# A long convolution beside attention on one core: two channels by 64 time shifts on the 128 rows of a filter tile, in place of one channel by 128

## The chip, the core and the metric

The kernel runs on one core of a Trainium2 chip. The metric is the device time of one execution in microseconds (us). In a profile, PE is the matrix engine, PEld its weight loads, DVE the vector engine, ACT the scalar engine, POOL the third compute engine and SP the engine that issues most DMAs. The profile counts 16 DMA engines for the core. "Granted clock" is the share of full clock that PE was allowed. SBUF is the core's working memory, whose tiles here have up to 128 partitions, PSUM the one that PE writes its results to. Repeated runs of one kernel lie up to some 1.5% apart (the fast runs of the kernel before, on the chip of runs 1 to 8, from 859.12 to 871.35 us), so effects of 1% rest on several runs of both kernels on the same chip, with a 95% interval; runs that were marked slow (over 1.5% above the fastest of the same kernel) are left out of the ratios.

## The reference, cut to what matters

Two independent halves, written side by side into one output:

```python
# A: attention, S = 2048, D = 512, 32 heads of 16
qkv = (x @ wqkv) ...
p = softmax(einsum("bhqd,bhkd->bhqk", q, k) * 16 ** -0.5)
a = einsum("bhqk,bhkd->bhqd", p, v) ... @ wo
# B: gated long convolution, 512 channels, filter as long as the sequence
k_shift = ...                     # k filtered in time with 4 taps per channel
kv = k_shift * v
y  = irfft(rfft(kv, 2 * S) * rfft(ssm_k, 2 * S))[:S]     # causal convolution along time
y  = y + kv * ssm_D
b  = q * y
return concatenate([a, b], axis=-1)
```

The kernel does the convolution without an FFT, as matrix products with Toeplitz matrices of the filter. The inputs are small random numbers, and the comparison with the reference is tolerant, so it cannot vouch for the values of the convolution. Where a variant is called correct below, that is by its construction.

## The kernel before

The kernel gives every engine a fixed stream of instructions, and a small model in the kernel's own Python decides the order. A score block is 128 keys by 512 queries. Of 2048 blocks ACT exponentiates 1835 and DVE 213 with a polynomial. Convolution matmuls are slipped between the score matmuls. The model books each DMA at 400 KB per us, plus 3.6 us:

```python
def dma(eng, dsem, outp, inp, deps=(), transpose=False, kb=512):
    h = dsem.add()
    start = max(eng.t, at(*deps))
    dma_t[0] = max(dma_t[0] + kb / DMA_KB, start + 3.6 + kb / DMA_KB)   # DMA_KB = 400
    done[(id(h[0]), h[1])] = dma_t[0]
    ...
```

The filters, reversed and padded with 128 zeros, lie in a DRAM scratch `kz` with one row of LKZ = 2176 elements per channel. A load gives partition p the row shifted by p elements, which makes the Toeplitz tile of a channel. One load serves a quad of four channels:

```python
WR = sb("WR", [128, 12, S])                  # 12 filter rows of 4 KB per partition: 3 slots of 4
KV = sb("KV", [128, C // 4, NB, 4])          # k*v by 128-blocks of time, NB = 16
...
src = bass.AP(tensor=kz_ap.tensor, offset=kz_ap[4 * qd, 0].offset,
              ap=[[1, 128], [LKZ, 4], [1, S]])            # [step, count], outermost first
h_wr[qd] = dma(sp, d_wr[i], WR[:, 4 * i:4 * i + 4, :], src, [h_kzw[0], dep], kb=2048)
...
def conv_lags(qd, n0, n1):                   # 16 lags of 128 times
    for n in range(n0, n1):
        for c in range(4):
            e.matmul(PS[32 * c:32 * c + NB - n, ...], lhsT=KV[:, qd, n:NB, c],
                     rhs=WR[:, r + c, 128 * (NB - 1 - n):128 * (NB - n)],
                     start=(n == 0), stop=(n == NB - 1), tile_position=(0, 32 * c))
    ...
    if n1 == NB:                             # the quad is done: its slot is free, load the next one
        wr_free.append((wr_slot[qd], h))
        load_wr()
```

An access pattern here is a list of [step, count] pairs, the outermost first.

The softmax here doesn't subtract the row's maximum and nothing guards it: scores larger than these inputs give would overflow.

## Time and profile before

| | before |
|---|---|
| time, three runs | 865.52 us (863.67 to 869.0) |
| span of the profiled run | 863.0 us |
| ACT busy | 837.7 us, 97% |
| DMA, MB moved by SP's queue | 279.33 |

ACT fills the span, and the DMA engines are nearly as full once the convolution runs (a share of 0.99 from 200 to 850 us, below). The prediction shows the lines for that. Two more views are used later. The first is from the page: the queue that carries the filter rows (packets, MB, share of the 16 engines' time), and the chain of work that ended last, by engine.

```profile
q1 hardware_dynamic: 93280, 279.33, 84.9%
...
ACT 56%; DMA 21%; PE 12%; DVE 8%; issue 1%; SPq 1%; ACTq 0%
```

The second is ACT's exponentials by stage: the stretch in us, its length, ACT's busy time in exponentials with their count, granted clock, DMA share of 16 engines, GB/s. Before 44 us the filter is prepared, up to 200 us the projections and k*v products are slipped in, and after that convolution and attention run side by side.

```profile
0.00:44.00 44.00, 33.59 (x30) 1.00 1.07 271
44.00:200.00 156.00, 155.30 (x151) 0.99 0.49 172
200.00:850.00 650.00, 639.57 (x557) 0.98 0.99 385
```

Since ACT is the bound, a change is judged by what ACT gets done in each stage. Ten us are lost in the first, only 0.7 in the second, and 10.4 in the third.

### The profile page before, as it was taken

What the parts mean: (1) busy time and instruction counts of PE and PEld (TensorE: products, weight loads), DVE (VectorE), ACT (ScalarE), POOL (GpSimd) and SP (SyncE); (2) the same over time, 40 slices, a digit from 0 to 9 for tenths busy, and PEclk for the clock granted to TensorE, in tenths of its full rate; (3) what the DMA queues carried; (4) which work ended last, traced back from release to release, by engine and by line L of the source; (5) the groups of instructions that cost most, each with busy time, mean ns of one, the idle gap of its engine ahead of it and who ended that gap; (6) DMA issues with size and microseconds to landing.
All of it is one profiled execution on the core that took longest, in us unless ns stands there. A gap on an engine that the chain in (4) does not pass through costs nothing.

```text
span 863.0 us, 29010 instructions
## 1 busy us (share of the span) xinstructions
PE 742.5 (86%) x13170; PEld 301.2 (35%) x13170; DVE 782.5 (91%) x1330; ACT 837.7 (97%) x746; POOL 17.3 (2%) x33
## 2 busy tenths in 40 slices
PE   8988999998888888888888888888888888788876
PEld 2223343443333333333333333333333333333332
DVE  3228999999999999999999999999999989999992
ACT  6999999999999999999999999999999999999997
POOL 2000000000000000000000001000000000000000
PEclk9999999999999999999999999999999999999999
DMA  9960067779999999999999999999999999999972
GB/s 272 269 221 1 1 198 246 261 246 355 407 375 369 404 409 407 405 378 408 407 394 378 407 406 388 356 375 362 385 396 408 406 387 373 392 401 373 408 297 74
DMA packets 98666, 289.31 MB, mean 335 GB/s; under 512 B 29040, under 2 KB 31088, under 8 KB 98160
## 3 DMA queue, kind: packets, MB, share of 16 engines
q1 hardware_dynamic: 93280, 279.33, 84.9%
q0 software_dynamic: 1808, 6.29, 2.2%
q8 instruction: 104, 1.70, 0.8%
q10 hardware_dynamic: 3456, 1.84, 0.7%
q14 instruction: 18, 0.15, 0.0%
HBM read 276.83 MB, written 6.42 MB: 328 GB/s over the span
## 4 chain that ended last, share of the span: by engine, by line
ACT 56%; DMA 21%; PE 12%; DVE 8%; issue 1%; SPq 1%; ACTq 0%
ACT PT L545 56%; DMA WR<-kz_scratch 20%; PE PS L534 5%; DVE EH L588 3%; PE PS L798 3%; PE PS L627 2%; DVE FX L581 1%; DVE PTD L593 1%; DMA WR<-in_B_ssm_D_dram 1%; SPq L218 1%; DVE QT L375 1%; PE PS L744 1%; PE PS L330 0%; PE PS L1004 0%; PE PS L358 0%
## 5 line engine op out<-in xcount | busy, mean ns | idle before, releaser
L545 ACT ACTIVATE PT<-PS 128x1536 bf16<-128x1536 f32 (+1 forms) x741 | 834.6, 1334 | 12.7 <-PE PS L534 11.7
L534 PE MATMUL PS<-QT,KTo 32*128 32x512 bf16 x2048 | 304.1, 388 | 86.9 <-ACT PT L545 69.0
L588 DVE SCALAR_TENSOR_TENSOR EH<-EH,FX 128x512 f32<-128x512 f32 x426 | 282.7, 682 | 0.1
L798 PE MATMUL PS<-WR,KV 128*16 128x128 bf16 (+15 forms) x8192 | 220.7, 222 | 18.1 <-DMA WR<-kz_scratch 16.0
L627 PE MATMUL PS<-PT,VAF 128*32 128x512 bf16 x1835 | 203.8, 393 | 3.7 <-DVE DT L691 2.1
L798 PEld LDWEIGHTS PS<-WR,KV 128*13 128x13 bf16 (+15 forms) x8192 | 148.9, 88 | 102.8 <-issue 40.2
L534 PEld LDWEIGHTS PS<-QT,KTo 32*128 32x128 bf16 x2048 | 73.0, 91 | 268.2 <-ACT PT L545 228.9
L581 DVE TENSOR_SCALAR FX<-PS 128x512 f32<-128x512 f32 x213 | 146.0, 685 | 7.5 <-PE PS L534 6.9
L593 DVE SCALAR_TENSOR_TENSOR PTD<-EH,FX 128x512 uint16<-128x512 f32 x213 | 144.1, 679 | 0.0
L588 DVE SCALAR_TENSOR_TENSOR EH<-FX 128x512 f32<-128x512 uint16 x213 | 143.2, 684 | 0.0
L627 PEld LDWEIGHTS PS<-PT,VAF 128*32 128x32 bf16 x1835 | 49.0, 93 | 120.8 <-issue 105.3
L1004 PE MATMUL PS<-IDN,ZW 128*32 128x512 bf16 (+3 forms) x221 | 70.7, 320 | 0.9 <-issue 0.9
L627 PE MATMUL PS<-PTD,VAF 128*32 128x512 bf16 x213 | 62.2, 387 | 0.0
L400 DVE CAST VAF<-PS 128x512 bf16<-128x512 f32 x16 | 11.1, 691 | 27.9 <-PE PS L358 27.9
L691 DVE STREAM_TRANSPOSE DT<-PS 128x512 f32<-128x512 f32 x31 | 22.0, 711 | 14.1 <-PE PS L627 13.8
L1004 PEld LDWEIGHTS PS<-IDN,ZW 128*32 128x32 bf16 x221 | 21.6, 98 | 8.6 <-issue 8.1
L375 DVE TENSOR_SCALAR QT<-PS,MASK 128x512 bf16<-128x512 f32 x30 | 21.1, 746 | 3.5 <-PE PS L330 3.5
L813 DVE CAST YB<-PS 128x512 bf16<-128x512 f32 x32 | 21.9, 684 | 0.9 <-PE PS L798 0.7
L744 PE MATMUL PS<-WKV,OTN 128*128 128x512 bf16 x64 | 20.1, 392 | 1.2 <-DVE OTN L713 1.2
L358 PE MATMUL PS<-WKV,xT 128*128 128x512 bf16 x64 | 18.8, 384 | 2.3 <-DVE VAF L400 1.7
L339 PE MATMUL PS<-xT,WKV 128*128 128x512 bf16 (+1 forms) x64 | 18.2, 377 | 1.1 <-DVE QT L375 0.5
L330 PE MATMUL PS<-xT,WQ 128*128 128x512 bf16 x60 | 18.0, 384 | 0.2
(62 smaller groups left out, 197.0 us busy)
## 6 DMA issues: line engine op xcount, KB each, us to landing
WR<-kz_scratch SPq DMA_DIRECT2D x128, 2048.0 KB, 11.6
kz_scratch<-WR SPq DMA_DIRECT2D x1, 2176.0 KB, 8.5
WR<-in_B_v_dram SPq DMA_DIRECT2D x4, 512.0 KB, 7.5
QN<-in_B_q_dram POOLq DMA_DIRECT2D x2, 1024.0 KB, 10.8
out_dram<-QN POOLq DMA_DIRECT2D x2, 1024.0 KB, 8.7
out_dram<-OUTA POOLq DMA_DIRECT2D x12, 128.0 KB, 5.7
QN<-in_B_ssm_k_dram SPq DMA_DIRECT2D x1, 1024.0 KB, 6.5
QT<-in_B_ssm_k_dram SPq DMA_DIRECT2D x1, 1024.0 KB, 8.5
```

The source lines that it names most:

```text
L375: lambda e, par=par: e.tensor_scalar(QT[:, qb % 2, 2 * o + par, :], PS[:, bank, :], MASK[:, par:par + 1], None, ALU.mult),
L534: ins = e.matmul(PS[:, bank, :], lhsT=KTo[32 * s:32 * s + 32, g // 2, kt * 128:(kt + 1) * 128], rhs=QT[32 * s:32 * s + 32, qb % 2, g, :], ...
L545: h_exp[T] = act.op(lambda e: e.activation(PT[:, T % R_PT, 0:n * QB], PS[:, banks[0]:banks[0] + n, :].rearrange("p b f -> p (b f)"), ACT.E ...
L581: h_f = urgent(lambda e: e.tensor_scalar(fx, PS[:, bank, :], FIX_ADD, FIX_HI, ALU.add, ALU.min), [h, h_last.get(i - R_FX)], slack=0.6)
L588: st["h"] = dve.op(lambda e: e.scalar_tensor_tensor(eh, src, (A3, A2, A1)[j], frac, ALU.add, ALU.mult), [st["h"], h_last.get(i - R_EH), h_ ...
L593: lambda e: e.scalar_tensor_tensor(out16, eh, A4, fx, ALU.mult, ALU.add),
L627: ins = e.matmul(dst, lhsT=w, rhs=rhs, start=(k == 0), stop=(k == KT - 1), tile_position=(0, 32 * s))
L691: h_t = urgent(lambda e: e.transpose(out=dt, in_=PS[:, pvb(n), :]), [h] + before, slack=0.1, us=(0.63, 0.751))
L744: ins = e.matmul(PS[:, bank, :], lhsT=OTN[:, (4 * qb + o) % R_O, t * 128:(t + 1) * 128], rhs=WO[:, o, :], start=(o == 0), stop=(o == 3))
L798: ins = e.matmul(PS[32 * c:32 * c + NB - n, BGB, 128 * (kk % 4):128 * (kk % 4) + 128], lhsT=KV[:, qd, n:NB, c], rhs=WR[:, r + c, 128 * (NB ...
L813: hh = urgent(lambda e: e.tensor_copy(YB[:, half, :].rearrange("p (k i) -> p k i", k=4), src), [h, h_yb[0]], slack=0.3, us=V512)
L1004: pe.op(lambda e: e.matmul(PS[32 * s:32 * s + 32, pvb(n), 0:128 * k], lhsT=ZW[:, :], rhs=rhs, start=False, stop=False, tile_position=(0, 3 ...
```

## The change

The intent is to halve the bytes of the filter. A filter tile of 128 rows holds 128 shifts of one channel before, 64 shifts of two channels (c and c + 128) after. One matmul then serves two channels, there are 32 lags of 64 times in place of 16 of 128, and each row pair is fetched by one DMA. So that the channels do not mix, the stationary side (k*v) has twice as many columns, and each column is zero in the half of the partitions that belongs to the other channel; its elements lie 4 apart, that is 8 bytes, as before.

```diff
-R_W = 12
+R_W = 10
-    KV = sb("KV", [128, C // 4, NB, 4])
+    KVF = sb("KV", [128, NOCT, 2, 2 * NB, 4])            # NOCT = 64 octets of channels
+    h_kv0 = pool.op(lambda e: e.memset(KVF[:, :, :, :, :], 0.0), [h_vaf1], us=(14.0, 14.1))
+    h_kz0 = pool.op(lambda e: e.memset(KZS[:, :, S:S + PAD], 0.0), [h_kv0])
...
-            h_kvc[c] = hh = urgent(lambda e: e.tensor_tensor(dst, src, val, ALU.mult), ...)
+            for p in range(2):                           # two products on 64 partitions each
+                dst = KV[64 * p:64 * p + 64, ...]
+                h_kvc[c] = hh = urgent(lambda e, ...: e.tensor_tensor(dst, src, val, ALU.mult), ...)
...
-            src = bass.AP(..., offset=kz_ap[4 * qd, 0].offset, ap=[[1, 128], [LKZ, 4], [1, S]])
-            h_wr[qd] = dma(sp, d_wr[i], WR[:, 4 * i:4 * i + 4, :], src, [h_kzw[0], dep], kb=2048)
+            row = 256 * (x // (2 * NOCT)) + x % (2 * NOCT)
+            src = bass.AP(..., offset=kz_ap[row, 0].offset, ap=[[128 * LKZ, 2], [1, 64], [1, S]])
+            h_wr[x] = dma(sp, d_wr[i], WR[:, i, :], src, [h_kzw[0], dep])
...
-                               lhsT=KV[:, qd, n:NB, c],
-                               rhs=WR[:, r + c, 128 * (NB - 1 - n):128 * (NB - n)],
+                               lhsT=KVF[:, od, lag % 2, 2 * q:32, c],
+                               rhs=WR[:, rows[c], w0:w0 + w],
```

Cut are the layout of v and of the copies of y, their smaller transposes, the order of the early units, and the ring of output tiles (4 to 3).

More of the change, by code (lines that the diff above doesn't have):

```diff
@@ L24 @@
 C = 512
+NOCT = C // 8
+NLAG = 32
+LAG_ORDER = [0, -1] + list(range(1, NLAG - 1))
 NB = S // 128
@@ L29 @@
 LKR = LEFT + S
-R_W = 12
+R_W = 10
 R_PT = 5
 R_O = 8
-R_A = 4
+R_A = 3
 CHB = 32
@@ L168, in bass_concat_heads__mha_block__ssm_conv_h3__prompt_kernel @@
     WRF = WR[:, :, :].rearrange("p r w -> p (r w)")
-    KV = sb("KV", [128, C // 4, NB, 4])
+    KVF = sb("KV", [128, NOCT, 2, 2 * NB, 4])
+    KV = KVF[:, :, :, :, :].rearrange("p k r (e h) c -> p r e h k c", h=2)
     QNF = sb("QN", [128, NB * 256 + 2 * LEFT])
@@ L180, in bass_concat_heads__mha_block__ssm_conv_h3__prompt_kernel @@
     OUTA = sb("OUTA", [128, R_A, D])
-    YB = sb("YB", [128, 2, 512])
+    YB = sb("YB", [128, 512])
     IDN = sb("IDN", [128, 128])
@@ L191, in bass_concat_heads__mha_block__ssm_conv_h3__prompt_kernel @@
     WO = WV
-    VST = WR[:, 8:12, :].rearrange("p c (t d) -> p c t d", t=NB)
+    VST = WR[:, 6:10, :].rearrange("p c (r e d) -> p c r e d", r=1, e=NB).rearrange("p (c r) o e d -> p c (r o) e d", r=2)
     KZS = WRF[:, 0:4 * LKZ].rearrange("p (c m) -> p c m", c=4)
@@ L259, in bass_concat_heads__mha_block__ssm_conv_h3__prompt_kernel @@
     d_outA = [DmaSem(sem(f"d_outA{i}")) for i in range(R_A)]
-    d_wr = [DmaSem(sem(f"d_wr{i}")) for i in range(R_W // 4)]
+    d_wr = [DmaSem(sem(f"d_wr{i}")) for i in range(R_W)]
     wview = A_wqkv.rearrange("(c p) f -> p c f", p=128)
@@ L283, in bass_concat_heads__mha_block__ssm_conv_h3__prompt_kernel @@
     h_vn, h_kt, h_kt0 = [], {}, {}
-    for c in range(4):
-        src = bass.AP(tensor=v2.tensor, offset=v2[128 * (NB - 1), 128 * c].offset, ap=[[D, 128], [-128 * D, NB], [1, 128]])
-        h_vn.append(dma(sp, d_kv[2 + c], VST[:, c, :, :], src, kb=1024))
+    for c in range(2):
+        for r in range(2):
+            for h in range(2):
+                src = bass.AP(tensor=v2.tensor, offset=v2[128 * (NB - 1) + 64 * r, 256 * c + 128 * h].offset,
+                              ap=[[D, 64], [-128 * D, NB], [1, 128]])
+                ld = dma(sp, d_kv[2 + 2 * c + r], VST[64 * h:64 * h + 64, c, r, :, :], src, kb=512)
+            h_vn.append(ld)
     def load_kt(i, dep):
@@ L305, in bass_concat_heads__mha_block__ssm_conv_h3__prompt_kernel @@
     h_vaf1 = pool.op(lambda e: e.memset(VAF[:, :, H * VW:VROW], 1.0))
-    h_kz0 = pool.op(lambda e: e.memset(KZS[:, :, S:S + PAD], 0.0))
+    h_kv0 = pool.op(lambda e: e.memset(KVF[:, :, :, :, :], 0.0), [h_vaf1], us=(14.0, 14.1))
+    h_kz0 = pool.op(lambda e: e.memset(KZS[:, :, S:S + PAD], 0.0), [h_kv0])
     act.op(lambda e: e.activation(JNK[:, 1:2], JNK[:, 0:1], ACT.Exp), [h_j], inc=False)
@@ L317, in unit_deps @@
         if u[0] == "kv":
-            return [h_kt[u[1] // 2], h_dg[0]]
+            return [h_kt[u[1]], h_dg[0]]
         return h_x[u[1] // 4] + [h_wv]
@@ L342, in pe_unit @@
             _, c, i = u
-            deps += [h_kt[c // 2], h_kt0[c // 2], h_dg[0]]
-            mm_us, mm_run = 0.27, 0.21
+            deps += [h_kt[c], h_kt0[c], h_dg[0]]
+            mm_us, mm_run = 0.25, 0.21
             def mm(e, b):
@@ L348, in mm @@
                 for m in range(4):
-                    c0 = LEFT + 128 * (4 * i + 3 - b) - m
-                    ins = e.matmul(PS[:, bank, 128 * b:128 * b + 128], lhsT=KTR[c // 2][:, c % 2, c0:c0 + 128], rhs=DG[:, c, m, :],
-                                   start=(m == 0), stop=(m == 3))
+                    for h in range(2):
+                        c0 = LEFT + 128 * (NB - 1 - 4 * (i % 4) - b) + 64 * (i // 4) - m
+                        ins = e.matmul(PS[64 * h:64 * h + 64, bank, 128 * b:128 * b + 128], lhsT=KTR[c][:, h, c0:c0 + 64],
+                                       rhs=DG[:, 2 * c + h, m, :], start=(m == 0), stop=(m == 3), tile_position=(0, 64 * h))
                 return ins
@@ L384, in evac_unit @@
             _, c, i = u
-            dst = KV[:, 32 * c:32 * c + 32, NB - 4 - 4 * i:NB - 4 * i, :]
-            val = VST[:, c, NB - 4 - 4 * i:NB - 4 * i, :].rearrange("p b (k c) -> p k b c", c=4)
-            src = PS[:, bank, :].rearrange("p (b k c) -> p k b c", b=4, c=4)
-            h_kvc[c] = hh = urgent(lambda e: e.tensor_tensor(dst, src, val, ALU.mult), [h, h_vn[c]], us=V512)
+            for p in range(2):
+                dst = KV[64 * p:64 * p + 64, i // 4, 4 * (i % 4):4 * (i % 4) + 4, p, 32 * c:32 * c + 32, :].rearrange("p e k c -> p k e c")
+                val = VST[64 * p:64 * p + 64, c, i // 4, 4 * (i % 4):4 * (i % 4) + 4, :].rearrange("p e (k c) -> p k e c", c=4)
+                src = PS[64 * p:64 * p + 64, bank, :].rearrange("p (e k c) -> p k e c", e=4, c=4)
+                h_kvc[c] = hh = urgent(lambda e, dst=dst, src=src, val=val: e.tensor_tensor(dst, src, val, ALU.mult),
+                                       [h, h_vn[2 * c + i // 4], h_kv0], us=V512)
             kv_n[c] += 1
-            if sum(kv_n[0:2]) == 8 and c < 2:
+            if c == 0 and kv_n[0] == 8:
                 load_qn(0, [h])
@@ L393, in evac_unit @@
                 h_kvm[0] = h
-                wr_free.append((2, hh))
+                wr_free.extend([(i, hh) for i in range(6, R_W)])
                 load_wr()
@@ L402, in evac_unit @@
         bank_free[bank] = hh
-    h_kvc = [None] * 4
-    kv_n = [0] * 4
+    h_kvc = [None] * 2
+    kv_n = [0] * 2
     h_kvm = [None]
@@ L428, in kz_store @@
         load_kt(1, h_kzt[0])
-        wr_free.extend([(i, h_kzw[0]) for i in range(2)])
+        wr_free.extend([(i, h_kzw[0]) for i in range(6)])
         load_wr()
@@ L769, in bass_concat_heads__mha_block__ssm_conv_h3__prompt_kernel, with wr_rows @@
     h_wr, h_qn = {}, {}
-    h_yb = [None]
-    h_ybw = [None]
+    h_yb, h_ybw = {}, {}
     wr_slot = {}
     def load_wr():
-        while wr_free and wr_next[0] < C // 4:
-            (i, dep), qd = wr_free.pop(0), wr_next[0]
+        while wr_free and wr_next[0] < 4 * NOCT:
+            (i, dep), x = wr_free.pop(0), wr_next[0]
             wr_next[0] += 1
-            wr_slot[qd] = i
-            src = bass.AP(tensor=kz_ap.tensor, offset=kz_ap[4 * qd, 0].offset, ap=[[1, 128], [LKZ, 4], [1, S]])
-            h_wr[qd] = dma(sp, d_wr[i], WR[:, 4 * i:4 * i + 4, :], src, [h_kzw[0], dep], kb=2048)
+            wr_slot[x] = i
+            row = 256 * (x // (2 * NOCT)) + x % (2 * NOCT)
+            src = bass.AP(tensor=kz_ap.tensor, offset=kz_ap[row, 0].offset, ap=[[128 * LKZ, 2], [1, 64], [1, S]])
+            h_wr[x] = dma(sp, d_wr[i], WR[:, i, :], src, [h_kzw[0], dep])
+    def wr_rows(od):
+        return [h_wr[4 * od + c] for c in range(4)]
     def load_qn(i, deps):
@@ L785, in load_qn, with conv_lags @@
                       q2[:, 256 * i:256 * i + 256].rearrange("(t p) d -> p t d", p=128), deps)
-    def conv_lags(qd, n0, n1):
-        kk = qd % 8
-        deps = [h_wr[qd], h_kvc[qd // 32]]
-        r = 4 * wr_slot[qd]
-        if kk % 4 == 0 and n0 == 0:
+    def conv_lags(od, n0, n1):
+        kk = od % 4
+        deps = wr_rows(od) + [h_kvc[2 * od // NOCT]]
+        rows = [wr_slot[4 * od + c] for c in range(4)]
+        if kk == 0 and n0 == 0:
             deps.append(bank_free[BGB])
@@ L796, in fn @@
             for n in range(n0, n1):
+                lag = LAG_ORDER[n]
+                q = (lag + 1) // 2
+                w0, w = 128 * NB - 128 - 64 * lag, 128 if lag >= 0 else 64
                 for c in range(4):
-                    ins = e.matmul(PS[32 * c:32 * c + NB - n, BGB, 128 * (kk % 4):128 * (kk % 4) + 128],
-                                   lhsT=KV[:, qd, n:NB, c],
-                                   rhs=WR[:, r + c, 128 * (NB - 1 - n):128 * (NB - n)],
-                                   start=(n == 0), stop=(n == NB - 1), tile_position=(0, 32 * c))
+                    ins = e.matmul(PS[32 * c:32 * c + 32 - 2 * q, BGB, 128 * kk:128 * kk + w],
+                                   lhsT=KVF[:, od, lag % 2, 2 * q:32, c],
+                                   rhs=WR[:, rows[c], w0:w0 + w],
+                                   start=(n == 0), stop=(n == NLAG - 1), tile_position=(0, 32 * c))
             return ins
@@ L804, in conv_lags @@
                   run=0.054 * (n1 - n0))
-        if n1 == NB:
-            wr_free.append((wr_slot[qd], h))
+        if n1 == NLAG:
+            wr_free.extend([(r, h) for r in rows])
             load_wr()
-            if kk % 4 == 3:
-                half = kk // 4
+            if kk == 3:
                 src = PS[:, BGB, :]
@@ L812, in conv_lags @@
                               ap=[src.ap[0], [128, 4], [-1, 128]])
-                hh = urgent(lambda e: e.tensor_copy(YB[:, half, :].rearrange("p (k i) -> p k i", k=4), src),
-                            [h, h_yb[0]], slack=0.3, us=V512)
-                bank_free[BGB] = h_ybw[0] = hh
+                hh = urgent(lambda e: e.tensor_copy(YB[:, :].rearrange("p (k i) -> p k i", k=4), src),
+                            [h, h_yb.get(od // 4 - 1)], slack=0.3, us=V512)
+                bank_free[BGB] = h_ybw[od // 4] = hh
         return h
@@ L822, in fn @@
             ins = None
-            for k in range(8):
-                ins = e.transpose(pbf[:, 128 * k:128 * k + 128], YB[:, k // 4, 128 * (k % 4):128 * (k % 4) + 128],
-                                  IDN[:, :])
-            return ins
-        h = pe.op(fn, [bank_free[bank], h_ybw[0], h_idn], us=(0.54, 0.681), run=0.43)
-        h_yb[0] = h
-        sl = b // 8
-        yv = pbf.rearrange("p (c j) -> p c j", j=32)[:, :, 0:NB].rearrange("p c j -> p j c")
-        yv = bass.AP(tensor=yv.tensor, offset=pbf[:, NB - 1:NB].offset, ap=[yv.ap[0], [-1, NB], [32, CHB]])
-        qv = QN[:, :, CHB * (b % 8):CHB * (b % 8) + CHB]
+            for k in range(4):
+                ins = e.transpose(pbf[:, 128 * k:128 * k + 128], YB[:, 128 * k:128 * k + 128], IDN[:, :])
+            return ins
+        h = pe.op(fn, [bank_free[bank], h_ybw[b], h_idn], us=(0.32, 0.46), run=0.215)
+        h_yb[b] = h
+        sl, b = b // 8, b % 8
+        yv = bass.AP(tensor=pbf.tensor, offset=pbf[:, 2 * NB - 2:2 * NB - 1].offset,
+                     ap=[pbf.ap[0], [-2, NB], [1, 2], [32, 16]])
+        qv = QN[:, :, :].rearrange("p t (h u) -> p t h u", h=2)[:, :, :, 16 * b:16 * b + 16]
         hh = urgent(lambda e: e.tensor_tensor(qv, yv, qv, ALU.mult), [h, h_qn[sl]], slack=0.3, us=V512)
         bank_free[bank] = hh
-        if b % 8 == 7:
+        if b == 7:
             dst = out2[:, D + 256 * sl:D + 256 * (sl + 1)].rearrange("(t p) c -> p t c", p=128)
@@ L847, in bass_concat_heads__mha_block__ssm_conv_h3__prompt_kernel @@
     early += [(91, ("k", 2, 0)), (92, ("q", 0, 2)), (98, ("k", 2, 1)), (104, ("k", 2, 2)), (110, ("k", 2, 3))]
-    early += [(130, ("kv", 1, i)) for i in range(4)]
+    early += [(130, ("kv", 0, i)) for i in range(4, 8)]
     early += [(137, ("q", 0, 3)), (138, ("k", 3, 0)), (144, ("k", 3, 1)), (150, ("k", 3, 2)), (155, ("k", 3, 3))]
-    early += [(N_EARLY - 4, ("kv", c, i)) for c in (2, 3) for i in range(4)]
+    early += [(N_EARLY - 4, ("kv", 1, i)) for i in range(8)]
     later_q = [("q", qb, o) for qb in range(1, NQB) for o in range(4)]
@@ L853, in bass_concat_heads__mha_block__ssm_conv_h3__prompt_kernel @@
     state = {"qd": 0, "lag": 0, "turn": False, "q": 0, "op": 0, "started": False, "lags": 0.0,
-             "left": C // 4 * NB, "t": 0.0}
+             "left": NOCT * NLAG, "t": 0.0}
     def room(T):
@@ L871, in next_unit @@
         if st["turn"]:
-            return T, ("turn", st["qd"] // 8 - 1)
+            return T, ("turn", st["qd"] // 4 - 1)
         jobs = []
@@ L875, in next_unit @@
             u = later_op[st["op"]]
-            jobs.append((NT * (u[0] + 2) // NQB - SLOT * 1, ("op",) + u))
+            jobs.append((NT * (u[0] + 2) // NQB - SLOT, ("op",) + u))
         if st["q"] < len(later_q):
@@ L896, in unit_step @@
             free = max(pe.t, at(bank_free[bank]) + 0.13)
-            if T < N_EARLY and st["turn"] and not part[0] and fits(T, free, 0.54):
-                conv_turn(st["qd"] // 8 - 1, bank)
+            if T < N_EARLY and st["turn"] and not part[0] and fits(T, free, 0.33):
+                conv_turn(st["qd"] // 4 - 1, bank)
                 st["turn"] = False
@@ L914, in unit_step @@
                 free = max(free, at(*unit_deps(u)) + 0.13)
-            if not fits(T, free, 0.54 if u[0] == "turn" else 0.645 if u[0] == "kv" else 0.535):
+            if not fits(T, free, 0.33 if u[0] == "turn" else 0.645 if u[0] == "kv" else 0.535):
                 if T < due or forced and N_EARLY <= T < stop:
@@ L945, in emit_bg @@
             load_wop(pe_last())
-        if not st["started"] and kv_n[0] == 4:
+        if not st["started"] and kv_n[0] == 8:
             st["started"] = True
         if T in tail_mm:
-            assert st["qd"] == C // 4 and not st["turn"], (T, st)
+            assert st["qd"] == NOCT and not st["turn"], (T, st)
             for t, g in tail_mm[T]:
@@ L952, in emit_bg @@
             return
-        if st["qd"] == C // 4 and not st["turn"] and st["op"] == len(later_op):
+        if st["qd"] == NOCT and not st["turn"] and st["op"] == len(later_op):
             if T < min(tail_mm):
@@ L956, in emit_bg @@
             return
-        if st["turn"] and st["qd"] == C // 4:
-            conv_turn(C // 32 - 1, BGB)
+        if st["turn"] and st["qd"] == NOCT:
+            conv_turn(NOCT // 4 - 1, BGB)
             st["turn"] = False
@@ L966, in emit_bg @@
         left = min(LAGS, int(st["lags"]), int((room(T) - 0.06) / 0.055))
-        while left > 0 and st["qd"] < wr_next[0] and kv_n[st["qd"] // 32] == 4 and at(h_wr[st["qd"]]) + WAIT <= pe.t:
-            if st["turn"] and st["qd"] % 4 == 3 and st["lag"] + left >= NB:
-                left = NB - 1 - st["lag"]
+        while left > 0 and 4 * st["qd"] + 3 < wr_next[0] and kv_n[2 * st["qd"] // NOCT] == 8 \
+                and at(*wr_rows(st["qd"])) + WAIT <= pe.t:
+            if st["turn"] and st["qd"] % 4 == 3 and st["lag"] + left >= NLAG:
+                left = NLAG - 1 - st["lag"]
                 if left <= 0:
@@ L974, in emit_bg @@
                 break
-            n1 = min(n0 + left, NB)
+            n1 = min(n0 + left, NLAG)
             left -= n1 - n0
@@ L979, in emit_bg @@
             conv_lags(st["qd"], n0, n1)
-            st["lag"] = n1 % NB
-            if n1 == NB:
+            st["lag"] = n1 % NLAG
+            if n1 == NLAG:
                 st["qd"] += 1
                 if st["qd"] % 4 == 0:
-                    st["turn"] = st["turn"] or st["qd"] % 8 == 0
+                    st["turn"] = True
                     break
@@ L1030, in bass_concat_heads__mha_block__ssm_conv_h3__prompt_kernel @@
         advance(pe.t)
-    assert state["qd"] == C // 4 and not state["turn"] and state["q"] == len(later_q) and state["op"] == len(later_op), state
+    assert state["qd"] == NOCT and not state["turn"] and state["q"] == len(later_q) and state["op"] == len(later_op), state
     assert not early_dve and not flow and not acts and not dves
```

## The prediction

> **What bounds the kernel now.** I read the page's busy shares first, then its 40 slices, then the groups by shape, then the waits.
>
> ```profile
> PE 742.5 (86%) x13170; PEld 301.2 (35%) x13170; DVE 782.5 (91%) x1330; ACT 837.7 (97%) x746; POOL 17.3 (2%) x33
> ...
> DMA  9960067779999999999999999999999999999972
> GB/s 272 269 221 1 1 198 246 261 246 355 407 375 369 404 409 407 405 378 408 407 394 378 407 406 388 356 375 362 385 396 408 406 387 373 392 401 373 408 297 74
> ...
> L545 ACT ACTIVATE PT<-PS 128x1536 bf16<-128x1536 f32 (+1 forms) x741 | 834.6, 1334 | 12.7 <-PE PS L534 11.7
> ```
>
> ACT, which takes the exponentials of the attention, is busy 837.7 of 863.0 us. Its 741 exponentials cover 834.6 us, with 12.7 us idle ahead of them. So ACT is the bound, and beside it a second one is all but reached: from slice 10 on the 16 DMA engines are 90% busy or more, at about 400 GB/s. These are the convolution's filter rows:
>
> ```profile
> WR<-kz_scratch SPq DMA_DIRECT2D x128, 2048.0 KB, 11.6
> ```
>
> 128 loads of 2 MB are 268 MB. At 408 GB/s they need 658 us, which just fits between the first filter load at 43.7 us and the last at 825.7. What the filter loads cost ACT stands in the waits (who waits, for whom, us in total, times, longest):
>
> ```profile
> ACT PT L545 <- PE PS L534: 11.7, 26, 0.9
> ...
> PE PS L798 <- DMA WR<-kz_scratch: 16.0, 27, 1.3
> ```
>
> [...]When a convolution matmul (L798) waits for a row, the score matmuls (L534) behind it are late and ACT idles. **At most some 11 us can be had by making the rows cheaper**: 863 to about 852 us, 1.3%, as long as ACT keeps its 1835 blocks (the other 213 go to DVE).
>
> Two rates are needed below: one DMA engine's speed, from stretches in which all 16 are saturated (columns: PE, PEld, DVE, ACT, POOL busy with counts, granted clock, DMA share, GB/s), and the start of the filter stream.
>
> ```profile
> 230.00:240.00 10.00, 8.23 (x143) 3.53 (x143) 10.00 (x18) 10.00 (x10) 0.00 (x0) 1.00 1.02 408
> ...
> 400.00:410.00 10.00, 8.31 (x184) 3.64 (x176) 9.92 (x18) 10.00 (x10) 0.00 (x0) 1.00 1.03 408
> ```
>
> ```profile
> 43.66 64.43 SPq L218 DMA_DIRECT2D WR<-kz_scratch  x3
> ```
>
> ```profile
> 131.29 1.32 POOL L218 DMA_DIRECT2D QN<-in_B_q_dram  x1 [110.62 <-PE PS L350]
> ```
>
> 408 GB/s over 16 engines is 25.5 GB/s each, so one 4 KB row of one partition takes an engine 4096 / 25.5 = 160.6 ns. The stretch 110 to 120 us, with the engines half busy (0.50) at 180 GB/s, has 180 / (16 x 0.50) = 22.5 GB/s per busy engine: an engine does not get faster when others are idle.[...] The last line is issued when the eighth k*v unit is done (L350), at 131 us; the changed kernel lets the convolution start after its eighth unit.
>
> [...]
>
> ```profile
> L798 PEld LDWEIGHTS PS<-WR,KV 128*16 128x16 bf16 x512 | 14.6, 93 | 33.6 <-DMA WR<-kz_scratch 28.8 <-issue 2.9
> ...
> L798 PEld LDWEIGHTS PS<-WR,KV 128*1 128x1 bf16 x512 | 14.2, 83 | 5.0 <-issue 3.3
> ```
>
> 93 against 83 ns for 15 more columns: 0.67 ns each.
>
> **The change part by part.**
> Arithmetic. Before: 128 quads x 16 lags x 4 = 8192 matmuls of 128 columns. After: 64 octets x 32 lags x 4 = 8192 again (the one at lag -1 is half as wide). Nothing is saved on PE. The stationary side grows from 8.5 to 17 columns on average; 32 columns would take 93 + 16 x 0.67 = 104 ns, overlapped with the matmuls before it. Small.
> DVE. The 16 k*v products become 32 of the same 512 elements per lane (+16 x 0.687 = +11.0 us). The copies into YB fall from 32 to 16 (-16 x 0.684 = -10.9 us). Sum 0, so about 213 blocks stay on DVE and ACT's work is unchanged.
> POOL. One more memset of 16384 elements; 1024 took 1.009 us and 256 took 0.304, so 0.92 ns each and 15 us, from about 3.4 to 18.5 us. The filter scratch is written at 33.5 us: hidden.
> PE transposes 128 -> 64, of 220 ns latency in groups: hidden.
> **The filter loads.** 256 loads of 512 KB in place of 128 of 2 MB: 134 MB. Were they spread over 16 engines, they would need 329 us of a span of over 700, and the waits of L798 would go. But look at the source pattern: before it is 128 partitions x 4 rows x 2048; after it is [2 channels][64 shifts][2048], so that one DMA serves both channels. Its slowest dimension is **2**, the tile's is 128[...]
> One load is 128 partition rows, 64 on each engine: 64 x 160.6 ns = **10.28 us** (on 16 engines 1.28 us). Six rows are free at the start; they land from 44 to 44 + 6 x 10.28 = 106 us, before the convolution wants them. The next load can only be issued when the first octet has freed its rows: 131 us plus some 10 us for 32 lags, 141 us. From then on at least six of the ten rows are outstanding at almost any time, so the two engines do not rest: 250 x 10.28 = 2570 us, until 2711 us. Other traffic after that (about 4 MB of output and 2 MB of q over 16 engines, 0.4 MB on each of the two) adds 0.4 MB / 25.5 GB/s = 16 us: 2727 us. Then the last octet (32 lags at 6 for each exponential of 1.14 us, 7 us) and the tail, which is 22 us now (last convolution matmul at 840.5, end at 863): 2727 + 7 + 22 = 2756, say **2760 us**.
> None of it is hidden. The order of the instruction streams was fixed by a model that books these loads at 400 KB per us; on the chip PE stops at the head of each octet until its fourth row has landed, about 4 x 10.28 - 10 = 31 us, with scores and exponentials behind it.
>
> **The rivals.**
> A. The loads do spread over 16 engines (the split is not taken from the source's outer 2, or the program reorders it). Then the DMA share falls to about half, the 16.0 us of PE waits go, and ACT's idle time shrinks by perhaps 8 of its 11.7 us: 855 us, -1.2%, "same". For it: the author books full rate; both sides hold 128 rows in all.[...]
> B. Spread, but PE becomes late: [...] Against: four loads of 32 columns at L627 cover 0.10 us together in the timeline, so different column groups load side by side.
> C. Two engines, but faster than 25.5 GB/s each when 14 rest.[...] Against: the 22.5 GB/s of the half-idle stretch.
>
> **Range and chances.** I give the two-engine case 0.87,[...] and 0.13 to A and B together (same mostly, 2% gain hardly: ACT's own work is 834.6 us). Within the two-engine case the only large factor is ns per packet: 150 to 175 ns gives 2590 to 2990. Range 2560 to 3020. Faster 0.02, same 0.10, slower 0.88.
>
> **What would show it.** DMA share near 2/16 = 0.12 for most of the span, about 51 GB/s; 256 filter loads with a median time to landing of several times 10 us[...]; L798's wait for the filter rows the largest of PE's waits, some 60 waits of about 30 us, near 1900 us in all; ACT busy still about 835 us, now 30% of the span; granted clock often at half after each stop. Wrong would be: a filter load that lands in 3 to 6 us with the DMA share near 0.5 (A), or PE waits that end in the weight loads (B).

Cut from it, at the marks, are a remark on the order in which PE works, a figure that the lines above it show, the reasons given for two engines per load and against rival A, what rivals B and C would come to, and the words that set the slope of the weight loads against another figure. The forecast's own sum: 141 us until the seventh load goes out, 250 loads of 10.28 us (2570), then 16, 7 and 22, together 2756, put down as 2760 us. The 160.6 ns for a 4 KB row were measured. That a load runs on two engines, and the next load on the same two, was the author's assumption; the trace before did not show it. The traces and runs below do.

## The result, and the profile after

| | before | after |
|---|---|---|
| time | 867.26 us (863.67 to 872.66, 4 runs) | 2754.93 us (2744.84 to 2755.88, 4 runs) |
| ratio | | 3.172 (3.153 to 3.192) |
| span of the profiled run | 863.0 | 2743.1 |

A ratio here and below is the mean time of one kernel's fast runs over that of the other's fast runs of the same rounds, so not quite the ratio of the medians shown. The changed kernel is slower by a factor of 3.2. The lines of its page that answer to those of before:

```profile
PE 903.5 (33%) x13388; PEld 352.8 (13%) x13388; DVE 798.2 (29%) x1330; ACT 863.3 (31%) x746; POOL 31.5 (1%) x34
...
GB/s 194 32 53 59 52 53 53 52 52 55 54 52 54 54 52 53 52 53 53 53 54 52 80 54 53 54 53 52 53 53 53 54 53 54 54 53 54 53 53 40
...
q1 hardware_dynamic: 59040, 145.10, 13.8%
...
DMA 77%; PE 15%; ACT 4%; DVE 2%; SPq 1%; issue 1%; ACTq 0%
...
L557 ACT ACTIVATE PT<-PS 128x1536 bf16<-128x1536 f32 (+1 forms) x741 | 860.2, 1253 | 1867.7 <-PE PS L546 1865.8
```

The bytes fell by half, and the rate to an eighth: about 53 GB/s in nearly every slice, where before there were 400. SP's queue uses 13.8% of the engines' time and yet the chain of work is DMA for 77%. The waits (who, for whom, us in total, times, longest) say who stood still:

```profile
ACT PT L557 <- PE PS L546: 1865.8, 248, 32.7
PE PS L816 <- DMA WR<-kz_scratch: 1778.2, 63, 32.8
```

63 waits of PE, about one for each of the 64 octets of channels, and ACT behind them. One such stop in stretches of 2 us (columns: PE, PEld, DVE, ACT, POOL busy with counts, granted clock, DMA share, GB/s), and four links of the chain of work (start, us, what):

```profile
1003.00:1005.00 2.00, 0.05 (x4) 0.00 (x0) 2.00 (x5) 1.15 (x2) 0.00 (x0) 1.00 0.13 51
1007.00:1009.00 2.00, 0.00 (x0) 0.00 (x0) 0.00 (x0) 0.00 (x0) 0.00 (x0) 0.50 0.13 51
...
1033.00:1035.00 2.00, 2.00 (x24) 0.86 (x23) 0.43 (x1) 1.45 (x2) 0.00 (x0) 0.50 0.13 53
```

```profile
957.08 34.14 DMA WR<-kz_scratch
...
998.07 33.52 DMA WR<-kz_scratch
...
1037.82 34.14 DMA WR<-kz_scratch
...
1078.81 33.51 DMA WR<-kz_scratch
```

PE has stopped at 1003 us, ACT and DVE run dry within 3 us of it, and PE resumes at 1031.7 us; the clock is halved in the stop and still half when PE resumes. Through all of it the DMA share stays at 0.13, two engines of 16. From 957.08 to 1078.81 are three octets of four loads: 121.73 / 12 = 10.14 us for a load. Read packet by packet from the trace, a 4 KB packet of the filter takes 160 ns (the middle one, as before; 161 on average), and two packets are in flight for 2463 of the 2743 us. So nothing became slow at one engine; 14 engines do nothing.

One line was not expected. The instruction that issues a filter load on SP's queue (duration ns: shortest, middle, longest; first and last start), before and after:

```profile
L218 SPq DMA_DIRECT2D WR<-kz_scratch x128: 359/359/582, 43.7 to 825.7; - x128
```

```profile
L222 SPq DMA_DIRECT2D WR<-kz_scratch x256: 482/9892/17014, 46.5 to 2663.6; - x128
```

0.36 us before, 9.9 us after: the issuing instruction itself is held for about as long as one load takes on two engines.

### The profile page after: what moved, and what is told of

The parts are those of the page before. It is cut to its first block, busy times and chain, and to the rows that moved or that the text cites. A ratio compares the mean times of both kernels' runs of the same rounds, so it can differ in the third digit from the quotient of the medians.

```text
span 2743.1 us, 29674 instructions
## 1 busy us (share of the span) xinstructions
PE 903.5 (33%) x13388; PEld 352.8 (13%) x13388; DVE 798.2 (29%) x1330; ACT 863.3 (31%) x746; POOL 31.5 (1%) x34
## 3 DMA queue, kind: packets, MB, share of 16 engines
q1 hardware_dynamic: 59040, 145.10, 13.8%
## 4 chain that ended last, share of the span: by engine, by line
DMA 77%; PE 15%; ACT 4%; DVE 2%; SPq 1%; issue 1%; ACTq 0%
DMA WR<-kz_scratch 77%; PE PS L546 5%; PE PS L816 5%; ACT PT L557 4%; PE PS L639 3%; PE PS L1021 1%; SPq L222 1%; DVE EH L600 1%; DVE KV L399 0%; DVE FX L593 0%; PE PS L360 0%; DMA WR<-in_B_ssm_D_dram 0%; DVE PTD L605 0%; PE PS L756 0%; PE PS L368 0%
## 5 line engine op out<-in xcount | busy, mean ns | idle before, releaser
L557 ACT ACTIVATE PT<-PS 128x1536 bf16<-128x1536 f32 (+1 forms) x741 | 860.2, 1253 | 1867.7 <-PE PS L546 1865.8
L816 PE MATMUL PS<-WR,KV 128*24 128x128 bf16 (+8 forms) x8192 | 298.2, 261 | 1779.4 <-DMA WR<-kz_scratch 1778.2
L816 PEld LDWEIGHTS PS<-WR,KV 128*18 128x18 bf16 (+7 forms) x8192 | 195.3, 108 | 1913.4 <-issue 1889.4
L546 PE MATMUL PS<-QT,KTo 32*128 32x512 bf16 x2048 | 362.9, 462 | 39.7 <-ACT PT L557 22.3
L639 PE MATMUL PS<-PT,VAF 128*32 128x512 bf16 x1835 | 240.2, 459 | 5.4 <-DVE DT L703 4.3
L1021 PE MATMUL PS<-IDN,ZW 128*32 128x512 bf16 (+3 forms) x243 | 94.3, 388 | 0.0
L639 PE MATMUL PS<-PTD,VAF 128*32 128x512 bf16 x213 | 74.9, 471 | 0.0
L849 DVE TENSOR_TENSOR QN<-PS,QN 128x512 bf16<-128x512 bf16 x16 | 11.0, 685 | 129.6 <-PE PS L841 129.6
L1021 PEld LDWEIGHTS PS<-IDN,ZW 128*32 128x32 bf16 x243 | 28.5, 117 | 5.9 <-issue 5.8
L399 DVE TENSOR_TENSOR KV<-PS,WR 64x512 bf16<-64x512 f32 x32 | 22.0, 686 | 19.0 <-PE PS L360 18.4
```

The source lines that it names most:

```text
L399: h_kvc[c] = hh = urgent(lambda e, dst=dst, src=src, val=val: e.tensor_tensor(dst, src, val, ALU.mult), [h, h_vn[2 * c + i // 4], h_kv0], ...
L546: ins = e.matmul(PS[:, bank, :], lhsT=KTo[32 * s:32 * s + 32, g // 2, kt * 128:(kt + 1) * 128], rhs=QT[32 * s:32 * s + 32, qb % 2, g, :], ...
L557: h_exp[T] = act.op(lambda e: e.activation(PT[:, T % R_PT, 0:n * QB], PS[:, banks[0]:banks[0] + n, :].rearrange("p b f -> p (b f)"), ACT.E ...
L639: ins = e.matmul(dst, lhsT=w, rhs=rhs, start=(k == 0), stop=(k == KT - 1), tile_position=(0, 32 * s))
L816: ins = e.matmul(PS[32 * c:32 * c + 32 - 2 * q, BGB, 128 * kk:128 * kk + w], lhsT=KVF[:, od, lag % 2, 2 * q:32, c], rhs=WR[:, rows[c], w0: ...
L1021: pe.op(lambda e: e.matmul(PS[32 * s:32 * s + 32, pvb(n), 0:128 * k], lhsT=ZW[:, :], rhs=rhs, start=False, stop=False, tile_position=(0, 3 ...
```

## The experiments

The theory: the source's outermost count of 2 confines a load to two DMA engines, and everything else is a consequence. Rivals: (B) the new layout is slow in itself (wider weights, more semaphores, fewer rows of ring); (D) one DMA for two channels is slow for another reason than the count of engines. The reshaped kernel has a second question as well: why do the halved bytes not make it faster once the loads spread?

### 1. Two loads per pair

```diff
-            src = bass.AP(..., offset=kz_ap[row, 0].offset, ap=[[128 * LKZ, 2], [1, 64], [1, S]])
-            h_wr[x] = dma(sp, d_wr[i], WR[:, i, :], src, [h_kzw[0], dep])
+            for h in range(2):
+                src = bass.AP(..., offset=kz_ap[row + 128 * h, 0].offset, ap=[[1, 64], [1, S]])
+                h_wr[x] = dma(sp, d_wr[i], WR[64 * h:64 * h + 64, i, :], src, [h_kzw[0], dep], kb=256)
```

> The changed kernel with each filter row pair loaded by two DMAs of 64 partitions (outermost count 64 on both sides) in place of one. Theory (the outer count 2 confines a load to two engines): 16 engines again, 855 us (845 to 870), DMA share about half in the steady stretch, PE's wait for filter rows under 20 us in all instead of 1778. Rival (the new layout itself, with 32-column weights and two channels on the rows, makes PE late): well over 900 us, with waits that end in weight loads or matmuls.

884.88 us (877.98 to 890.32, 6 runs), ratio 1.022 (1.016 to 1.028): 1870 us are gone, with the new layout in place and correct. It is still 2% slower than before, outside the expected 845 to 870. The waits of convolution matmuls for filter rows have shrunk to 0.2 us; three more waits before them, 7.7 us in all, are listed as "issue", that is without a releaser that the profile shows. But the DMA engines are unexpectedly full, which run 8 takes up.

### 2. The same load with the two dimensions of the source exchanged

```diff
-ap=[[128 * LKZ, 2], [1, 64], [1, S]]
+ap=[[1, 64], [128 * LKZ, 2], [1, S]]
```

Wrong: the channels alternate from partition to partition, where the products expect them in halves. All instruction streams, bytes, packets of 4 KB, semaphores and waits are those of the changed kernel.

> The changed kernel with one DMA for each row pair still, the same bytes and the same number of 4 KB packets, but the two dimensions of the source swapped: [64 shifts][2 channels][2048] in place of [2][64][2048]. The result is wrong on purpose (the rows land on other partitions). Every instruction on every other engine is the same. Theory: the outermost count is 64[...], so 16 engines: 850 to 870 us. Rival (one DMA over two separate stretches of the source, or its issue on the SP queue, is what is slow): about 2750 us.

869.87 us (868.60 to 871.18, 4 runs), ratio 1.005 (1.000 to 1.011), the same as before. Its waits list no convolution matmul waiting for a row; ACT's wait for the scores is now

```profile
ACT PT L557 <- PE PS L546: 17.1, 27, 3.2
```

in place of 1865.8 us. That one exchanged line is worth 1885 us, so (B) and (D) fall: neither layout nor the single DMA is slow. What the expectation did not have is that 11.7 us of idle ACT before the change have become 17.1, although rows no longer hold up PE. Runs 6 and 10 take that up.

### 3 and 4. Outermost counts of 4 and 8

```diff
+ap=[[64 * LKZ, 4], [1, 32], [1, S]]      # run 3
+ap=[[32 * LKZ, 8], [1, 16], [1, S]]      # run 4
```

Wrong again (4 channels by 32 shifts, 8 by 16), with the same streams.

> One DMA for each row pair, the same bytes and packets, the source as [4 rows][32 shifts][2048]; wrong result on purpose. Theory: four engines, 32 packets x 160.6 ns = 5.14 us for a load in place of 10.28. 250 loads from 141 us on make 1285 us, with 16 for other traffic and 29 for the last octet and the tail 1471 us (1420 to 1530). Rival (the loss does not go with the outermost count): about 2750, or about 860.

> As the run before with the source as [8 rows][16 shifts][2048]; wrong result on purpose. Theory: eight engines, 2.57 us for a load, 10.3 us for an octet, which is close to the 9.4 to 11 us that the schedule gives an octet: the DMA stops being the bound, 860 to 910 us, with PE waits for filter rows of up to some 40 us. Rival as before: about 2750.

One run each, of unknown state: 1516.56 us and 977.73 us. Their waits for filter rows:

```profile
PE PS L816 <- DMA WR<-kz_scratch: 551.1, 63, 14.1
```

```profile
PE PS L816 <- DMA WR<-kz_scratch: 74.5, 29, 6.6
```

With 4 KB packets of 162.6 ns on average in run 3, 250 loads of 32 packets per engine take 1301 us; 1516 less that is 215 us for start and tail, where the changed kernel has 173 (2755 - 250 x 64 x 161.4 ns); the difference was not traced. Run 4 **missed** its expected 860 to 910. The middle packet is 161 ns, as in the changed kernel within 1 ns, but the mean is 185.6, so 250 x 16 x 185.6 ns = 742 us in place of 642, and the rows come late 29 times. Why the slowest twentieth takes over 306 ns with eight engines was not tried. What counts is the order of the four, and the number of packets that the traces show in flight: most often exactly 2 in the changed kernel (2463 of 2743 us), 4 in run 3 (1180 of 1515) and 8 in run 4 (576 of 976).

| outermost count of the source | time, us |
|---|---|
| 2 (the change) | 2754.93 |
| 4 | 1516.56 |
| 8 | 977.73 |
| 64 | 869.87 |

### 5. The changed loads from POOL's queue

```diff
-            h_wr[x] = dma(sp, d_wr[i], WR[:, i, :], src, [h_kzw[0], dep])
+            h_wr[x] = dma(pool, d_wr[i], WR[:, i, :], src, [h_kzw[0], dep])
```

The author assumed that a load issued by POOL keeps to two engines as well, but that successive loads go to different pairs and so overlap; no trace before this run had shown it. A passage on this is cut from the expectation.

> The changed kernel with the 256 filter loads issued from the POOL queue in place of the SP queue; source pattern, bytes and result unchanged. Theory (each load keeps to two engines[...]): a load still needs 10.3 us, but four to six are in flight on different pairs, so an octet waits some 2 us for its last row: 930 us (880 to 1000), PE's wait for filter rows 60 to 150 us. Rival (the POOL queue keeps to one pair too): about 2750 us. Rival (two engines are no matter of the pattern but of the SP queue): about 865.

1166.07 us, one run, correct: far from 2755, and from the 2596 us that 256 loads of 10.14 us would take one after the other, so loads do overlap, but more than the 880 to 1000 expected. Which engines each load took was not read from the trace. Packets are longer (208.6 ns on average) and the middle load lands in 16.1 us. The page, with the issuing instructions (mean ns of one) behind the convolution:

```profile
q0 software_dynamic: 268048, 141.44, 52.1%
...
L816 PE MATMUL PS<-WR,KV 128*24 128x128 bf16 (+8 forms) x8192 | 268.6, 243 | 238.6 <-DMA WR<-kz_scratch 235.6
L222 POOL DMA_DIRECT2D WR<-kz_scratch x256 | 200.6, 804 | 646.2 <-PE PS L816 379.2
```

The 268048 packets of the queue include 233744 of four bytes. Less the 272 that the runs with all filter loads on SP's queue have, that is 912 for each load; in run 7, whose POOL loads have 64 outermost, it is 16. Whether the longer packets, the extra ones or the issues on POOL cause the 235.6 us of waits stays open.

### 6. Run 2 with the zeroing of k*v moved

The changed kernel clears the k*v tile on POOL before anything else; here it is cleared after the filter has been handed over.

```diff
-    h_kv0 = pool.op(lambda e: e.memset(KVF[:, :, :, :, :], 0.0), [h_vaf1], us=(14.0, 14.1))
-    h_kz0 = pool.op(lambda e: e.memset(KZS[:, :, S:S + PAD], 0.0), [h_kv0])
+    h_kz0 = pool.op(lambda e: e.memset(KZS[:, :, S:S + PAD], 0.0))
...
         load_kt(1, h_kzt[0])
+        h_kv0[0] = pool.op(lambda e: e.memset(KVF[:, :, :, :, :], 0.0), [h], us=(14.0, 14.1))
```

> The run with the swapped source dimensions (16 engines, wrong result on purpose) and one thing more: POOL's zeroing of KV, 13.75 us from 3.5 us on, is issued after the filter scratch has been handed over (about 21 us) in place of ahead of it. Theory (the zeroing held up DVE's four copies by 2 us in the first 22 us, PE idled, its clock was halved for 10 us, and ACT lost 6.7 us of the first 44): ACT's busy time in the first 44 us comes back from 28.7 to 34 to 36 us and the time falls from 870 to about 863 (858 to 867). Rival (that stage loses for another reason, such as the eight loads of v in place of four): no change, 868 to 872.

868.90 us (863.13 to 877.60, 6 runs, two of them slow), ratio 1.001 (0.996 to 1.007): the same as before, and not told apart from run 2: the expected 858 to 867 is missed by the median, and the fast runs are on average 3.3 us below those of run 2, less than the intervals resolve. The stages do tell something. ACT's exponentials in run 2 and in run 6, one profiled run each, columns as above:

```profile
0.00:44.00 44.00, 26.86 (x23) 0.84 1.08 254
44.00:200.00 156.00, 151.55 (x144) 0.98 0.19 62
200.00:850.00 650.00, 645.53 (x567) 1.00 0.59 206
```

```profile
0.00:44.00 44.00, 33.54 (x30) 1.00 1.02 254
44.00:200.00 156.00, 150.75 (x144) 0.98 0.21 65
200.00:850.00 650.00, 645.48 (x566) 0.99 0.59 205
```

In the third stage ACT has 6.0 us more than before (645.5 against 639.6): the halved bytes, and perhaps the 16 copies of y that DVE saves there. Run 2 gives 6.7 of them back in the first stage and 3.7 in the second. The zeroing is the cause of the first loss: moved, it leaves 33.54, as before. Its size differs from run to run: the seven profiles of this document with the early zeroing have 26.9 to 30.2 us in this stage (29.2 or more in all but run 2), the four with the late one 31.4 to 33.5. So 6.7 us is the largest loss seen, and 3.4 to 4.4 the usual one. How it comes about is to be seen on POOL and DVE at 17 us (start, us, what), in the changed kernel, before, and in run 6:

```profile
3.48 13.75 POOL L314 MEMSET KV<- 128x16384 bf16 x1
...
17.28 0.52 POOL L315 MEMSET WR<- 128x512 bf16 x1
17.38 3.39 DVE L433 COPY WR<-QN 128x2048 bf16<-128x2048 bf16 x2 [2.24 <-DMA WR<-in_B_ssm_D_dram]
17.76 2.45 POOL L445 TENSOR_SCALAR_AFFINE_SELECT OTN<-SHK 128x2048 bf16<-128x2048 bf16 x1
```

```profile
17.39 1.29 DVE L421 COPY WR<-QN 128x2048 bf16<-128x2048 bf16 x2 [1.67 <-DMA WR<-in_B_ssm_D_dram]
```

```profile
17.43 1.29 DVE L433 COPY WR<-QN 128x2048 bf16<-128x2048 bf16 x2 [1.78 <-DMA WR<-in_B_ssm_D_dram]
...
20.80 13.75 POOL L441 MEMSET KV<- 128x16384 bf16 x1
21.21 0.69 DVE L412 CAST VAF<-PS 128x512 bf16<-128x512 f32 x1 [0.47 <-PE PS L368]
```

The 13.75 us do not themselves disturb DVE: in run 6 the casts from PSUM beside them take their usual 0.69 us. They push POOL's next two instructions to where DVE reverses the filter, and there the pair of copies takes 3.4 us in place of 1.3. That it is POOL's select beside them that slows the copies is the author's reading of these lines; no run here takes the select away alone. DVE is then two us late and PE with it (its projections wait 3.10 us for a cast at 21.5 us, against 0.69 in run 6): run 2 is granted 0.59 of the clock from 20 to 26 us and 0.50 from there to 32, before and run 6 all of it. In the changed kernel it is back at 0.86 from 25 to 30 us, and its loss is the smaller one of 3.9 us.

### 7. Two loads per pair from two queues

The halves of run 1, one from SP and one from POOL, each with its own semaphore, and the zeroing moved as in run 6. What the theory of this run and the next was built on is that a 4 KB packet took 271 ns on average in run 1, with 64 neighbouring partitions for each load, and 161 in the changed kernel; the mechanism behind it is not shown by any run and is cut from both expectations.

```diff
+            for h, eng in ((0, sp), (1, pool)):
                 src = bass.AP(..., offset=kz_ap[row + 128 * h, 0].offset, ap=[[1, 64], [1, S]])
+                ... dma(eng, (d_wr, d_wp)[h][i], WR[64 * h:64 * h + 64, i, :], src, ..., kb=256)
```

> A correct kernel: two loads of 64 partitions for each filter row pair, the half for partitions 0 to 63 from the SP queue and the half for 64 to 127 from the POOL queue, each on its own semaphore; the zeroing of KV late, as in the run before. Theory ([...]from two queues both halves are written at once): mean packet 160 to 220 ns, 858 to 872 us. Rival (the POOL queue hands its loads over too late or too slowly beside DVE): waits for rows as in the run with two loads from SP, 880 us or more.

936.33 us (925.52 to 938.34, 6 runs), ratio 1.079 (1.073 to 1.085): a **miss**, slower. Packets still take 250 ns (SP) and 260 ns (POOL), and POOL spends 518 ns on each of 256 issues. Issuing the halves from two queues hardly shortens a packet (271 in run 1). Convolution matmuls now wait 43.5 us before they start, 36.7 of it listed as "issue"; that fits the rival, late rows, but the releaser is not shown.

### 8. Run 1 with other partitions

Same streams, same 64 partitions per load, but every other one. Its output is wrong, which doesn't matter for the time.

```diff
-                h_wr[x] = dma(sp, d_wr[i], WR[64 * h:64 * h + 64, i, :], src, [h_kzw[0], dep], kb=256)
+                h_wr[x] = dma(sp, d_wr[i], WR[h:128:2, i, :], src, [h_kzw[0], dep], kb=256)
```

> The run with two loads of 64 partitions from the SP queue, with one thing changed: the first load writes partitions 0, 2, 4 and so on and the second 1, 3, 5 and so on, in place of 0 to 63 and 64 to 127; wrong result on purpose. Source, packets, number of loads and all instruction streams are the same. Theory[...]: mean packet back from 271 to about 165 ns, DMA share from 0.9 to about 0.6, 866 to 874 us. Rival (smaller loads, or twice as many, are what is slow): packets stay near 270 ns and the time at 880 to 890.

870.19 us (869.90 to 884.27, 4 runs, one slow), ratio 1.005 (0.998 to 1.013). A stretch of 100 us of run 1, then of run 8 (columns as in the stop above):

```profile
300.00:400.00 100.00, 87.22 (x1924) 39.29 (x1909) 99.78 (x171) 100.00 (x89) 2.20 (x4) 1.00 0.96 228
```

```profile
300.00:400.00 100.00, 86.77 (x1857) 38.77 (x1856) 99.35 (x170) 98.47 (x88) 2.19 (x4) 1.00 0.70 226
```

The same packets, the same rate, but 0.96 of the engines' time against 0.70 (over the whole run, 68.8% against 52.3% for SP's queue): a 4 KB packet takes 271 ns on average (middle 278) into 64 neighbouring partitions, and 197 (middle 159) into every other one. So it is the destination's partitions that slow the engines. Run 1 moves 228 GB/s in this stretch with the engines full; why neighbouring partitions are the slower ones was not shown. Issuing the halves from two queues did not lift it (run 7: 250 and 260 ns a packet, 206 GB/s at a share of 0.81 from 300 to 400 us).

### 9. Run 1 with the true rate in the model

The zeroing moved, and each half load booked so that the model's 400 KB per us becomes what the engines do.

```diff
-                h_wr[x] = dma(sp, ..., WR[64 * h:64 * h + 64, i, :], src, [h_kzw[0], dep], kb=256)
+                h_wr[x] = dma(sp, ..., WR[64 * h:64 * h + 64, i, :], src, [h_kzw[0], dep], kb=445)
```

> A correct kernel: two loads of 64 partitions for each filter row pair, both from the SP queue, the zeroing of KV late, and the loads booked in the model that orders the instruction streams at the 230 GB/s that such loads were seen to reach, in place of 400. Theory (the 15 us between the run with two loads and the run with the swapped source dimensions were rows that landed later than the model had booked, so that PE stood still): PE no longer meets rows that have not landed, ACT's waits for PE fall from 33.6 us to about 11, 862 to 870 us, the same as the kernel before. Rival (packets of 271 ns cost time in another way, by slowing the weights or the matmuls): 878 us or more.

877.11 us (867.55 to 889.62, 6 runs, one slow), before 867.63 in the same rounds, ratio 1.010 (1.003 to 1.017). That misses the expected 862 to 870, and is about half of run 1's excess; ACT's wait for scores falls from 33.6 to 21.5 us, not to the 11 hoped for. As the zeroing was moved as well, the part of the true rate in this is not shown alone. It is the fastest of the correct variants, and still no faster than the kernel before. The other half shows mostly in the third stage, where ACT has 638.2 us of exponentials against 645.5 in run 6; what causes it stays open.

### 10. Run 6 with one of the two k*v products

Wrong: 16 products in place of 32, as many as before. In its second stage run 6 still had 150.75 us of exponentials against 155.30.

```diff
-            for p in range(2):
+            for p in range(1):
```

> The run with the swapped source dimensions and the late zeroing, with the second of the two k*v products of each unit left out (16 in place of 32 on DVE; wrong result on purpose). Theory (ACT's loss of 4 to 5 us between 44 and 200 us, 150.75 against 155.30 in the kernel before, comes from the 16 products more that hold up DVE's other PSUM reads, and so the banks of the scores, ahead of 200 us): ACT's busy time there returns to 154 to 156 us, time some 4 us less, 859 to 866. Rival (it comes from the k*v matmuls themselves, 64 columns at a time, or from the half clock around 180 us): it stays at 150 to 152.

852.84 us (851.74 to 853.68, 4 runs), before 867.13, ratio 0.985 (0.981 to 0.989).

```profile
0.00:44.00 44.00, 32.85 (x29) 1.00 1.13 254
44.00:200.00 156.00, 155.55 (x151) 1.00 0.23 76
200.00:850.00 650.00, 642.93 (x564) 1.00 0.58 203
```

The second stage is whole again, so the 16 extra products are the second loss. The time fell below its expectation too (859 to 866): of the 10.3 us between the profiled spans of run 6 and run 10 the second stage gives 4.8, and 2.9 come from less exponential work (831.3 us in all against 834.2; the model now gives DVE 215 blocks and ACT two fewer). So the 1.5% against the kernel before is not the worth of the halved bytes alone: run 10 also has 11 us less work on DVE than that kernel, 16 copies of y fewer and no products more, and no run separates the two. A 64-partition product costs what a 128-partition one does (686 against 687 ns, from the groups), so a correct kernel with this layout has to pay 32 of them or find another way to place the zeros.

## Why the prediction was right, point by point

- **Two engines per load.** Shown by run 2 (only the order of the source's dimensions differs), by the graded counts of runs 3 and 4, and by the packets in flight (2, 4 and 8). In the prediction it was an assumption, and nothing in the trace before could decide it.
- **10.28 us per load.** 10.14 measured. The engine's rate was taken from stretches with all 16 busy; with 14 idle a packet takes 161 ns on average, so rival C (faster engines) falls.
- **The first rows** had landed by 110 us (said 106). **The seventh load** went out at 156.3 us and not at 141: the first octet took from 139.7 to 156, since the lags are rationed per exponential. **The filter stream's end** is at 2697 us (said 2727): 250 loads in 2541 us, other traffic included, are 10.16 each, where the prediction had 2570 + 16. From there the last octet took 18 us to its last matmul at 2715.4 (said 7), and the tail 28 (said 22). These errors, +15, -45, +11 and +6, cancel, so that the sum hits closer (span 2743 against 2756, time 2755 against 2760) than its terms is luck; all of them together are under 3%.
- **Some 60 waits of about 31 us, near 1900 in all.** 63 waits, 1778.2 us, longest 32.8.
- **DMA share 0.12 at 51 GB/s, clock often at half.** 0.13, about 53, mean clock 0.629 in the profiled run. **ACT busy still 835 us** was low: 863.3, with the same 741 exponentials. It is as high in run 3 (862.8), and 837 to 841 in runs 1, 2, 6 and 8, which have no stops; why an exponential lengthens around a stop was not tried. The time from issue to landing, said to be several times 10 us, is not shown for these loads and stays unchecked.
- **Rival B** (wide weights): 32 columns load in 109 ns (said 104), and in run 2 the convolution matmuls wait for nothing but DVE's k*v products, 1.2 us. Not the cause.
- **The "hidden" POOL memset was wrong**, without harm to the number because the stops cover it. Its 15 us were right (13.75), hidden it was not: it moved other POOL work onto DVE's copies, 6.7 us of ACT in run 2 and 3.4 to 4.4 in the other profiles with it.
- **"DVE, sum 0" was right as a sum and wrong as an argument.** The 11 us added (k*v products) fall into the second stage, the 11 us saved (copies of y) mostly into the third. Run 10, without them, has the 3.7 to 4.6 us back that were lost there.
- **Rival A's 855 us**, what the change would give with spread loads, was therefore too low: run 2 gives 870. The gain itself was sized well (said 8 us; in the third stage ACT has 6.0 more, not all of it surely from the bytes), but the two items above give it back.

## What to carry to other kernels

Before a load is reshaped, read the outermost count of both its access patterns: with 2, 4 or 8 on one side and 128 on the other a load ran on 2, 4 or 8 of 16 engines here, and the DMA share in the trace, flat at 0.13 with two, shows it at a glance; put a dimension such as the 64 of run 2 or the 128 of the kernel before outermost, or, with care for the destination's partitions (271 ns a packet into 64 neighbouring ones, 197 into every other one), cut the load. Halved bytes only pay for as much as waits for bytes cost, here 16 us of PE waits and 6 us of ACT. And add up an engine's added and saved work by stage, not over the whole kernel.

## What else the runs measured

- The issuing instruction of a filter load on SP's queue is held for 9.9 us (the middle one) when successive loads share two engines, 4.8 with four (run 3), where a load takes 10.1 and 5.2; 0.6 with eight (run 4) or 16 (run 2), and 0.36 in the kernel before.
- The middle 4 KB packet took 160 to 161 ns, about 25.5 GB/s, whether 16 engines were busy (the kernel before) or two (the changed kernel).
- Cutting a load into two halves of 64 neighbouring partitions has a cost of its own: a packet takes 271 ns (run 1) in place of 197 into every other partition (run 8).
- Loads from POOL's queue with 2 outermost carry extra four-byte packets, 912 for each load (run 5), where in run 7 a load with 64 outermost carries 16. What they cost no run here separates.
- Weight loads of the convolution in run 2: two columns take 83 ns and 32 take 109, that is 0.87 ns for each column more.
